# One core, S4D convolution beside a gated linear unit: the sums of two chunks of the convolution's kernels in one block of matmuls, the Fourier stage behind it, and a second Ft buffer in place of the negated sines

## The chip, the core and the metric

The kernel runs on one core of a Trainium2 chip. A core has TensorE (PE, with a separate row PEld for its weight loads), VectorE (DVE), ScalarE (ACT), GpSimd (POOL) and the queue engine SyncE (SP); each takes its instructions in a fixed order, and they wait for each other through semaphores. The metric is the device time of one execution in microseconds; three executions before the change gave a median of 730.58 us.

## The reference

With x = A_u (2048 tokens, 448 channels) and xn = layernorm(x), the result is x + A(xn) + B(xn):

```python
# A: S4D, N = 256 complex modes per channel
dt = exp(log_dt); A = -exp(log_A_real) + 1j * A_imag
C = (C_real + 1j * C_imag) * dt[:, None]
P = exp((A * dt[:, None])[:, :, None] * arange(L))
K = 2 * einsum("dn,dnl->dl", C, P).real          # a kernel of 2048 taps per channel
y = irfft(rfft(K, 2L) * rfft(u, 2L))[:L] + u * D_skip
# B: GLU
h = sigmoid(xn @ w_gate) * (xn @ w_up)           # 448 -> 1792
out_B = h @ w_down                               # 1792 -> 448
```

## The kernel before

Two streams of work share the engines. One, `glu`, is part B: 14 tiles of 128 hidden columns for two halves of the tokens, each tile a `gate` step (two groups of 11 matmuls into `gu`, then tanh `th` on ACT, `hf` on DVE, its rounded copy `hh` on ACT and the rest `hl` on DVE), and after each two or three tiles the down projection (matmuls into `po`, added into `acc` by DVE). The other, `conv`, is part A: preparation, then `kgen`, which makes the convolution kernels, then `spectra`, the Fourier products. The two are written out in turn by a table of weights (a generator yields its weight, and the one that is behind goes on); a scheduler then lays down a fixed order for each engine, in which `issue_after` puts kgen's matmuls behind the gate or down matmul written last.

The change lies in `kgen`. It works on 56 chunks of 8 channels. For a chunk, a kernel is the product of a coarse factor F (32 steps) and a fine factor E (64 steps), summed over the 256 modes (two halves of 128 partitions) and over the real and imaginary parts. For each chunk, in turn:

- `ahead`: two matmuls with `sel` make the phases in a PSUM tile `tr` (one buffer). ACT turns them into the tile S: an absolute value (L541), the sines of E and F (L542), the negated sine of E (L543, half as wide), and the cosines (L544). S has two buffers, by the chunk's parity. `ahead` of chunk c+1 is written ahead of the products of chunk c.
- `magnitudes`: POOL makes the decays `me` and `mf` for a pair of chunks in 11 products (L499, L511) out of the powers `pm` (DVE, L447); ACT squares a part (L524).
- DVE multiplies: L598 the upper 32 steps of Et, L599 the lower 32 steps, for which S is read backwards (cosine and negated sine), L600 the tile Ft. Et has two buffers by parity, Ft has one.
- 32 matmuls with Ft as weights and Et as the moving operand (L614) sum a chunk into the PSUM bank `ko`. A bank takes four chunks. The profile records each of these matmuls twice, so a chunk shows as x64.
- Once a bank is full, a matmul with `dm` adds the skip term (L624), ACT copies the bank to `ks` (L627), and `first_stage` (32 matmuls into `kp` and `kq`, L559, recorded twice as well) makes its first Fourier stage, which goes to memory as `sk_d`. With chunks counted from 0, banks fill at chunks 3, 7, 11 and so on, and their first stages are written behind chunks 6, 10, 14 and so on; the last bank's behind the last chunk.

Of the kernel before, what the change touches and what calls it, by code (L numbers as in the profile page):

```python
# [11 lines left out]
F32 = mybir.dt.float32  # L12
F32R = mybir.dt.float32r
I32 = mybir.dt.int32
AF = mybir.ActivationFunctionType
ALU = mybir.AluOpType
# [10 lines left out]
TWO_PI = 2.0 * math.pi  # L27
# [9 lines left out]
HP = 300  # L37
# [10 lines left out]
DC = 8  # L48
# [81 lines left out]
def s4d_glu_kernel(ctx, tc, io):  # L130
# [322 lines left out]
    def kgen(pk):  # L453
# [5 lines left out]
            ("S1", [128, 5, 2 * DC, 32], F32), ("Et1", [128, 2, 2 * DC, 64], F32),  # L459
            ("Et0", [128, 2, 2 * DC, 64], F32), ("Ft", [128, 2, 2 * DC, 32], F32),  # L460
            ("S0", [128, 5, 2 * DC, 32], F32), ("mf0", [128, 4 * DC, 32], F32),
# [64 lines left out]
        def ahead(cn):  # L526
# [13 lines left out]
            cs = S[:, 1:4:2]  # L540
            nc.scalar.activation(rows(cs), pv, AF.Abs)  # L541
            nc.scalar.activation(rows(S[:, 0:5:4]), pv, AF.Sin, scale=TWO_PI)  # L542
            nc.scalar.activation(rows(S[:, 2:3]), pv[:, :, 0:1], AF.Sin, scale=-TWO_PI)  # L543
# [34 lines left out]
        for g in range(NCK // NCH):  # L578
            for c in range(NCH):
# [16 lines left out]
                Ft = tl["Ft"]  # L596
                two = lambda ap: ap.unsqueeze(1).to_broadcast([128, 2, 2 * DC, 32])
                v.tensor_tensor(Et[:, :, :, 32:64], two(me[:, :, 32:64]), S[:, 1::-1], ALU.mult)  # L598
                v.tensor_tensor(Et[:, :, :, 0:32], two(me[:, :, 0:32]), S[:, 1:3, :, ::-1], ALU.mult)  # L599
                fts[:] = [v.tensor_tensor(Ft, two(mf), S[:, 3:5], ALU.mult)]  # L600
# [7 lines left out]
                with tc.issue_after(glu_mm[0].ins):  # L608
                    for q in range(2):
                        sl = 2 * (cn % 4) + q  # L610
                        for k in range(4):
                            h, cc = k // 2, k % 2
                            for j in range(4):
                                nc.tensor.matmul(  # L614
                                    ko[32 * j : 32 * j + 32, sl],
                                    Ft[:, cc, DC * h + 4 * q + j],
                                    Et[:, cc, DC * h + 4 * q + j],
                                    start=(k == 0),
                                    stop=(k == 3),
                                    skip_group_check=True,  # L620
                                )
                if cn % 4 == 3:
# [4 lines left out]
                    nc.scalar.copy(ks, ko)  # L627
                yield WK / 3
                if cn % 4 == 2 and cn > 3 or cn + 1 == NCK:

                    with hp(HP) if cn + 1 == NCK else tc.issue_after(glu_mm[0].ins):
                        first_stage((cn - 3) // 4 if cn + 1 < NCK else cn // 4)
# [527 lines left out]
```

## Time and profile before

| what | value |
|---|---|
| median of three runs | 730.58 us (728.54 to 733.38) |
| the profiled execution, own time | 727.83 us |
| its span, first to last instruction | 726.1 us |
| mean granted TensorE clock | 0.980 |
| busy: PE, PEld, DVE | 677.6, 533.8, 565.7 us |
| busy: ACT, POOL | 420.6, 384.2 us |
| matmuls of kgen's sums (L614) | from 148.1 to 536.7 us |

Busy shares are of the engine's own records. A matmul's record overlaps the next one's, so what a matmul costs is read from the distance between starts, not from its duration. What lies before 140 us is preparation and gate work, what lies behind 540 us is `spectra` with the rest of the GLU.

### The profile page before, as it was taken

The page shows a single profiled execution, that of the slowest core. Times are in us where ns is not written, and L with a number is a line of the kernel's source. Part 1 is how long each engine was busy: PE and PEld are TensorE (multiplying, and loading weights), DVE is VectorE, ACT ScalarE, POOL GpSimd, SP SyncE. Part 2 cuts the span into 40 slices and gives each one's busy share as a digit, 9 for nine tenths or more (in the row PEclk, how much of TensorE's full clock was granted, in tenths as well). Part 3 has the DMA queues.
Part 4 walks back from the last instruction along what each step waited for, and adds up shares of the span by engine and source line. Part 5 has one row for each costly group of instructions (what it writes and reads, how often), then busy time and mean ns, then how long its engine had stood idle before and what let it go on. Part 6 is the DMA issues. An engine that isn't in the chain of part 4 may idle for free.

```text
span 726.1 us, 19068 instructions
## 1 busy us (share of the span) xinstructions
PE 677.6 (93%) x7780; PEld 533.8 (74%) x7780; DVE 565.7 (78%) x776; ACT 420.6 (58%) x650; POOL 384.2 (53%) x423
## 2 busy tenths in 40 slices
PE   2898799899998999998999999999999999999994
PEld 1674688787886888655778887888877787767783
DVE  5699997699999999999499988986956555664553
ACT  3645455578787788898388678767643312323310
POOL 2110018698899988788557856767844002431001
PEclk9998899999999999999999999999999999999998
DMA  9946328525414554454952232232269999999646
GB/s 203 229 108 183 104 80 248 164 93 177 167 51 135 185 158 147 135 162 130 270 183 102 83 108 97 71 108 94 58 172 271 273 235 234 233 244 221 166 131 162
DMA packets 92710, 115.71 MB, mean 159 GB/s; under 512 B 12112, under 2 KB 81104, under 8 KB 92368
## 3 DMA queue, kind: packets, MB, share of 16 engines
q1 hardware_dynamic: 83312, 94.03, 47.2%
q10 hardware_dynamic: 6736, 14.57, 6.4%
q0 software_dynamic: 2576, 5.90, 3.3%
q8 instruction: 61, 1.00, 0.6%
q14 instruction: 25, 0.20, 0.1%
HBM read 69.70 MB, written 44.76 MB: 158 GB/s over the span
## 4 chain that ended last, share of the span: by engine, by line
PE 58%; DVE 17%; POOL 8%; DMA 7%; issue 3%; ACT 3%; SPq 2%; ACTq 0%; POOLq 0%; DVEq 0%
PE gu L706 23%; PE po L818 12%; PE sp L902 7%; PE ko L614 5%; PE pv L929 4%; POOL me L511 4%; PE tr L533 3%; DVE Et L599 2%; DVE Et L598 2%; DVE Ft L600 2%; DVE hl L724 2%; POOL mf L511 2%; DMA acc_d<-acc 1%; DVE wl L761 1%; DVE pm L447 1%
## 5 line engine op out<-in xcount | busy, mean ns | idle before, releaser
L511 POOL TENSOR_TENSOR me<-me,pm 128x32 f32<-128x32 f32 (+1 forms) x168 | 155.9, 928 | 78.1 <-DVE Et L599 65.5
L511 POOL TENSOR_TENSOR mf<-mf,pm 128x64 f32<-128x64 f32 (+1 forms) x112 | 116.5, 1040 | 4.9
L706 PE MATMUL gu<-xh,wh 128*128 128x512 f32 x336 | 101.1, 407 | 2.5 <-ACT xh L219 2.5
L706 PE MATMUL gu<-xh,wl 128*128 128x512 f32 x336 | 95.4, 392 | 0.0
L706 PE MATMUL gu<-xl,wh 128*128 128x512 f32 x336 | 95.1, 390 | 0.0
L818 PE MATMUL po<-dh,hh 128*128 128x448 f32 x224 | 86.8, 387 | 6.0 <-DVE acc L823 2.5
L598 DVE TENSOR_TENSOR Et<-me,S 128x1024 f32<-128x1024 f32 x56 | 81.8, 1460 | 7.2 <-ACT S L544 5.5
L599 DVE TENSOR_TENSOR Et<-me,S 128x1024 f32<-128x1024 f32 x56 | 79.3, 1415 | 7.8 <-ACT me L524 7.7
L818 PE MATMUL po<-dl,hh 128*128 128x448 f32 x224 | 84.5, 377 | 0.0
L541 ACT ACTIVATE S<-tr 128x1024 f32<-128x1024 f32 x56 | 57.8, 1032 | 45.3 <-PE tr L533 40.3
L600 DVE TENSOR_TENSOR Ft<-mf,S 128x1024 f32<-128x1024 f32 x56 | 78.7, 1405 | 6.8 <-ACT S L544 5.0
L818 PE MATMUL po<-dh,hl 128*128 128x448 f32 x224 | 83.7, 375 | 0.0
L706 PEld LDWEIGHTS gu<-xh,wh 128*128 128x128 f32 x336 | 62.3, 193 | 21.3 <-ACT xh L219 4.0
L722 ACT CAST hh<-hf 128x512 fp32r<-128x512 f32 x56 | 35.0, 625 | 70.0 <-DVE hf L717 57.6
L706 PEld LDWEIGHTS gu<-xh,wl 128*128 128x128 f32 x336 | 62.9, 188 | 14.9 <-DVE pl L307 0.7
L706 PEld LDWEIGHTS gu<-xl,wh 128*128 128x128 f32 x336 | 63.0, 188 | 13.9 <-issue 0.7
L614 PEld LDWEIGHTS ko<-Et,Ft 128*32 128x32 f32 x3584 | 53.8, 110 | 25.7 <-issue 14.7
L614 PE MATMUL ko<-Et,Ft 128*32 128x64 f32 x3584 | 63.9, 222 | 7.6 <-DVE Ft L600 4.2
L717 DVE SCALAR_TENSOR_TENSOR hf<-th,gu 128x512 f32<-128x512 f32 x56 | 38.2, 682 | 38.4 <-PE gu L706 28.0
L544 ACT ACTIVATE S<-S,hpi 128x1024 f32<-128x1024 f32 x56 | 65.7, 1173 | 0.0
L823 DVE SCALAR_TENSOR_TENSOR acc<-po,acc 128x448 f32<-128x448 f32 x80 | 48.5, 616 | 21.7 <-PE po L818 21.7
L724 DVE TENSOR_TENSOR hl<-hf,hh 128x512 fp32r<-128x512 f32 x56 | 51.2, 915 | 13.2 <-ACT hh L722 13.2
(196 smaller groups left out, 1286.5 us busy)
## 6 DMA issues: line engine op xcount, KB each, us to landing
sk_d<-sk ACTq DMA_DIRECT2D x14, 512.0 KB
sx<-x_d SPq DMA_DIRECT2D x32, 224.0 KB
skl<-sk_d SPq DMA_DIRECT2D x16, 448.0 KB
vp<-v_d SPq DMA_DIRECT2D x16, 448.0 KB
v_d<-vt SPq DMA_DIRECT2D x62, 112.0 KB
wt_d<-wh SPq DMA_DIRECT2D x9, 512.0 KB
wt_d<-wl SPq DMA_DIRECT2D x9, 512.0 KB
wl<-wt_d SPq DMA_DIRECT2D x9, 512.0 KB
```

The lines of the kernel that those rows point to most:

```text
L511: ins = nc.gpsimd.tensor_tensor(m[:, :, w + a : 2 * w : n], m[:, :, a:w:n], par(base + i).unsqueeze(2).to_broadcast([128, 4 * DC, w // n]) ...
L541: nc.scalar.activation(rows(cs), pv, AF.Abs)
L544: sins[:] = [nc.scalar.activation(cs, cs, AF.Sin, scale=-TWO_PI, bias=hpi)]
L598: v.tensor_tensor(Et[:, :, :, 32:64], two(me[:, :, 32:64]), S[:, 1::-1], ALU.mult)
L599: v.tensor_tensor(Et[:, :, :, 0:32], two(me[:, :, 0:32]), S[:, 1:3, :, ::-1], ALU.mult)
L600: fts[:] = [v.tensor_tensor(Ft, two(mf), S[:, 3:5], ALU.mult)]
L614: nc.tensor.matmul(ko[32 * j : 32 * j + 32, sl], Ft[:, cc, DC * h + 4 * q + j], Et[:, cc, DC * h + 4 * q + j], start=(k == 0), stop=(k == ...
L706: glu_mm[:] = [nc.tensor.matmul(ps, a_, b_, start=(n == 0), stop=(n == len(mm) - 1))]
L724: v.tensor_tensor(hl, hf, hh, ALU.subtract)
L818: glu_mm[:] = [nc.tensor.matmul(po, a_[:, bs], w_, start=(n == 0), stop=(n == 3 * fc - 1))]
L823: v.scalar_tensor_tensor(acc[:, b], po, 0.5, acc[:, b], ALU.mult, ALU.add)
L902: mm = nc.tensor.matmul(to, tb[:kk, t, 64 * c : 64 * c + 64], rhs, start=True, stop=True, skip_group_check=True,)
```

## The change

Four edits, all in kgen. The sines: S has four slots instead of five, and the negated sine is gone from ACT; the lower half of Et is made in two instructions, one product with the cosine and one `scalar_tensor_tensor` with the sine and a factor -1. Ft gets two buffers by parity, like Et. The matmuls of the sums are written only behind an odd chunk, for the even chunk before it and for itself. The first Fourier stage of a bank is written right behind the block that sums the first two chunks of the next bank, under the same anchor; the last bank's stays where it was.

```diff
-            ("S1", [128, 5, 2 * DC, 32], F32), ("Et1", [128, 2, 2 * DC, 64], F32),
-            ("Et0", [128, 2, 2 * DC, 64], F32), ("Ft", [128, 2, 2 * DC, 32], F32),
-            ("S0", [128, 5, 2 * DC, 32], F32), ("mf0", [128, 4 * DC, 32], F32),
+            ("S1", [128, 4, 2 * DC, 32], F32), ("Et1", [128, 2, 2 * DC, 64], F32),
+            ("Et0", [128, 2, 2 * DC, 64], F32), ("Ft0", [128, 2, 2 * DC, 32], F32), ("Ft1", [128, 2, 2 * DC, 32], F32),
+            ("S0", [128, 4, 2 * DC, 32], F32), ("mf0", [128, 4 * DC, 32], F32),
...
-            cs = S[:, 1:4:2]
+            cs = S[:, 1:3]
             nc.scalar.activation(rows(cs), pv, AF.Abs)
-            nc.scalar.activation(rows(S[:, 0:5:4]), pv, AF.Sin, scale=TWO_PI)
-            nc.scalar.activation(rows(S[:, 2:3]), pv[:, :, 0:1], AF.Sin, scale=-TWO_PI)
+            nc.scalar.activation(rows(S[:, 0:4:3]), pv, AF.Sin, scale=TWO_PI)
...
-                Ft = tl["Ft"]
+                Ft = tl[f"Ft{cn % 2}"]
                 two = lambda ap: ap.unsqueeze(1).to_broadcast([128, 2, 2 * DC, 32])
                 v.tensor_tensor(Et[:, :, :, 32:64], two(me[:, :, 32:64]), S[:, 1::-1], ALU.mult)
-                v.tensor_tensor(Et[:, :, :, 0:32], two(me[:, :, 0:32]), S[:, 1:3, :, ::-1], ALU.mult)
-                fts[:] = [v.tensor_tensor(Ft, two(mf), S[:, 3:5], ALU.mult)]
+                v.tensor_tensor(Et[:, 0, :, 0:32], me[:, :, 0:32], S[:, 1, :, ::-1], ALU.mult)
+                v.scalar_tensor_tensor(Et[:, 1, :, 0:32], me[:, :, 0:32], -1.0, S[:, 0, :, ::-1], ALU.mult, ALU.mult)
+                fts[:] = [v.tensor_tensor(Ft, two(mf), S[:, 2:4], ALU.mult)]
...
                 with tc.issue_after(glu_mm[0].ins):
-                    for q in range(2):
-                        sl = 2 * (cn % 4) + q
...
+                    for c_ in (cn - 1, cn) if cn % 2 else ():
+                        Et, Ft = tl[f"Et{c_ % 2}"], tl[f"Ft{c_ % 2}"]
+                        for q in range(2):
+                            sl = 2 * (c_ % 4) + q
...
+                if cn % 4 == 1 and cn > 3:
+                    with tc.issue_after(glu_mm[0].ins):
+                        first_stage((cn - 2) // 4)
                 yield WK / 3
-                if cn % 4 == 2 and cn > 3 or cn + 1 == NCK:
-
-                    with hp(HP) if cn + 1 == NCK else tc.issue_after(glu_mm[0].ins):
-                        first_stage((cn - 3) // 4 if cn + 1 < NCK else cn // 4)
+                if cn + 1 == NCK:
+                    with hp(HP):
+                        first_stage(cn // 4)
```

The order in which the instructions stand, at three places. In the rows, `ko` are the sums of a bank, `Et0` and `Et1` are the even and the odd chunk's tile, `tr` are the two phase matmuls of a later chunk, `gu` are gate matmuls; line numbers are those of each kernel's own text, so L614 before is L616 after, L706 is L710, and L598 to L600 before are L597 to L600 after, with L597 the upper half of Et, L598 and L599 the two lower parts and L600 Ft.

First place, TensorE in the second half of kgen, the odd chunk 49. Before, its sums stand alone between gate matmuls:

```order
L706 MATMUL gu_5392<-xl_3862,wh_5306 128x512 x3
L706 MATMUL gu_5436<-xh_3861,wh_5306 128x512 x3
L706 MATMUL gu_5436<-xr_3863,wh_5306 128x512
L706 MATMUL gu_5436<-xh_3861,wl_5307 128x512 x3
L706 MATMUL gu_5436<-xr_3863,wl_5307 128x512
L706 MATMUL gu_5436<-xl_3862,wh_5306 128x512 x3
L706 MATMUL gu_5488<-xh_3545,wh_5484 128x512
L614 MATMUL ko_5322<-Et1_1125,Ft_1127 32x64 x32
L533 MATMUL tr_5459<-sel_76,ph1_1133 128x512 x2
```

After, the same sums follow those of chunk 48, and the phases of chunk 50 stand five gate matmuls ahead of them:

```order
L710 MATMUL gu_5360<-xh_3897,wh_5306 128x512 x3
L710 MATMUL gu_5360<-xr_3899,wh_5306 128x512
L710 MATMUL gu_5360<-xh_3897,wl_5307 128x512 x2
L533 MATMUL tr_5348<-sel_76,ph1_1134 128x512 x2
L710 MATMUL gu_5360<-xh_3897,wl_5307 128x512
L710 MATMUL gu_5360<-xr_3899,wl_5307 128x512
L710 MATMUL gu_5360<-xl_3898,wh_5306 128x512 x3
L616 MATMUL ko_5322<-Et0_1126,Ft0_1127 32x64 x32
L616 MATMUL ko_5322<-Et1_1125,Ft1_1128 32x64 x32
```

What moved: the even chunk's sums went down by some 23 gate matmuls, to stand directly ahead of the odd chunk's.

Second place, TensorE after the change, one pair earlier (chunks 46 and 47 close a bank; `tr_5281` are the phases of the odd chunk 49):

```order
L616 MATMUL ko_4941<-Et0_1126,Ft0_1127 32x64 x32
L616 MATMUL ko_4941<-Et1_1125,Ft1_1128 32x64 x32
L626 MATMUL ko_4941<-dm_79,ident_69 128x8
L710 MATMUL gu_5260<-xh_3897,wh_5112 128x512 x3
L710 MATMUL gu_5260<-xr_3899,wh_5112 128x512
L710 MATMUL gu_5260<-xh_3897,wl_5113 128x512 x3
L710 MATMUL gu_5260<-xr_3899,wl_5113 128x512
L710 MATMUL gu_5260<-xl_3898,wh_5112 128x512 x3
L533 MATMUL tr_5281<-sel_76,ph0_1133 128x512 x2
```

What moved: before, the phases of a chunk stood a whole chunk ahead of its sums; now those of an odd chunk stand behind the previous pair's block and 11 gate matmuls, with 33 gate matmuls and one more pair of phases between them and the block that needs them.

Third place, VectorE in the first half of kgen, a pair of chunks whose decays are `me1` and `mf1` (`wl`, `hf`, `hl` belong to the GLU, `pm` are powers). Before:

```order
L599 TENSOR_TENSOR Et0_1126<-me1_1122,S0_1128 128x32x32
L761 TENSOR_TENSOR wl_3294<-wraw_2743,wh_3293 128x1024
L724 TENSOR_TENSOR hl_2733<-hf_2730,hh_2732 128x512
L598 TENSOR_TENSOR Et0_1126<-me1_1122,S0_1128 128x32x32
L600 TENSOR_TENSOR Ft_1127<-mf1_1123,S0_1128 128x1024
L447 SCALAR_TENSOR_TENSOR pm1_1180<-W1_110 128x128
L717 SCALAR_TENSOR_TENSOR hf_2822<-th_2820,gu_2808 128x512
L447 SCALAR_TENSOR_TENSOR pm1_1180<-pm1_1180 128x128
L598 TENSOR_TENSOR Et1_1125<-me1_1122,S1_1124 128x32x32
L599 TENSOR_TENSOR Et1_1125<-me1_1122,S1_1124 128x32x32
L724 TENSOR_TENSOR hl_2825<-hf_2822,hh_2824 128x512
L600 TENSOR_TENSOR Ft_1127<-mf1_1123,S1_1124 128x1024
```

After, from the GLU work behind the previous pair's last product on:

```order
L721 SCALAR_TENSOR_TENSOR hf_2460<-th_2458,gu_2446 128x512
L765 TENSOR_TENSOR wl_2708<-wraw_2485,wh_2707 128x1024
L728 TENSOR_TENSOR hl_2463<-hf_2460,hh_2462 128x512
L600 TENSOR_TENSOR Ft0_1127<-mf1_1123,S0_1129 128x1024
L447 SCALAR_TENSOR_TENSOR pm1_1180<-W1_110 128x128
L598 TENSOR_TENSOR Et0_1126<-me1_1122,S0_1129 128x16x32
L599 SCALAR_TENSOR_TENSOR Et0_1126<-me1_1122,S0_1129 128x16x32
L597 TENSOR_TENSOR Et0_1126<-me1_1122,S0_1129 128x32x32
L447 SCALAR_TENSOR_TENSOR pm1_1180<-pm1_1180 128x128
L721 SCALAR_TENSOR_TENSOR hf_2619<-th_2617,gu_2605 128x512
L599 SCALAR_TENSOR_TENSOR Et1_1125<-me1_1122,S1_1124 128x16x32
L728 TENSOR_TENSOR hl_2622<-hf_2619,hh_2621 128x512
```

What moved: Ft of the even chunk now opens the pair, behind GLU work (`hf`, `wl`, `hl`) that follows the last product of the pair before; it is the instruction that waits for TensorE to have read the even half of the previous block. A chunk takes four instructions instead of three.

22 lines of the change are left out of this document (11 added, 11 removed).

## The prediction

> **What bounds the kernel now.** I read the page first: which engine is full, and which work the chain that ended last passes through.
>
> ```profile
> span 726.1 us, 19068 instructions
> ...
> PE 677.6 (93%) x7780; PEld 533.8 (74%) x7780; DVE 565.7 (78%) x776; ACT 420.6 (58%) x650; POOL 384.2 (53%) x423
> ...
> PE 58%; DVE 17%; POOL 8%; DMA 7%; issue 3%; ACT 3%; SPq 2%; ACTq 0%; POOLq 0%; DVEq 0%
> ```
>
> TensorE is the bound of the whole, but a quarter of the chain is on DVE and POOL, so I ask where. The chain restricted to four stretches of kgen (140 to 232, 232 to 290, 290 to 372, 372 to 537 us) gives these shares by line:
>
> ```profile
> by line: POOL me L511 26.1%; POOL mf L511 12.9%; DVE Et L599 8.4%; issue 8.2%; DVE hl L724 8.1%; DVE Et L598 7.7%; DVE Ft L600 5.7%; POOL dl L788 4.6%; DVE pm L447 4.4%; DVE wl L761 4.1%; DVE hf L717 3.4%; DMA rd<-in_B_w_down_dram 3.0%; POO
> by line: PE gu L706 39.9%; PE po L818 19.9%; PE ko L614 14.9%; PE tr L533 8.4%; DVE Ft L600 4.4%; PE kp L559 3.6%; DVE hl L724 2.7%; DVE Et L598 2.2%; issue 1.8%; DVE hf L717 1.2%; DVE xt L268 1.1%; PE gu L210 1.0%; PE ko L624 0.6%; PE kq L
> by line: DMA acc_d<-acc 12.0%; DVE Et L599 10.5%; PE gu L706 8.9%; DVE Ft L600 8.8%; DVE Et L598 8.2%; PE ko L614 6.7%; issue 5.3%; PE po L818 5.2%; DVE pm L447 4.4%; PE gu L279 4.1%; DMA wl<-wt_d 4.0%; PE tr L533 3.0%; PE gu L210 2.3%; DVE
> by line: PE gu L706 41.4%; PE po L818 23.9%; PE ko L614 13.9%; PE tr L533 8.1%; PE kq L559 2.2%; PE kp L559 2.0%; DVE Et L598 1.2%; PE ko L624 1.2%; DVE Ft L600 1.1%; DVE Et L599 1.1%; ACT S L544 0.6%; ACT S L541 0.6%; ACT S L542 0.6%; issu
> ```
>
> The first and third stretch run over DVE and POOL, the second and fourth over TensorE. The busy times of the same stretches say how near the others are:
>
> ```profile
> core 0: us, PE busy (x) PEld busy (x) DVE busy (x) ACT busy (x) POOL busy (x), PEclk, DMA share, GB/s
> 140.00:232.00 92.00, 88.17 (x1239) 71.91 (x1237) 88.24 (x88) 71.25 (x104) 84.58 (x79) 1.00 0.36 122
> 232.00:290.00 58.00, 57.35 (x884) 47.20 (x887) 55.79 (x58) 47.05 (x68) 50.37 (x51) 0.97 0.50 157
> 290.00:372.00 82.00, 75.85 (x1180) 53.19 (x1168) 67.78 (x79) 64.78 (x106) 57.72 (x67) 0.98 0.60 181
> 372.00:537.00 165.00, 163.93 (x2504) 135.97 (x2502) 141.37 (x143) 119.32 (x171) 117.08 (x131) 1.00 0.32 100
> ```
>
> In the first stretch DVE is busy 88.24 of 92 us and POOL 84.58: nothing can be added there unpaid. In the last, TensorE is busy 163.93 of 165 us and DVE has 23.6 us to spare. The stretches hold 12, 9, 11 and 24 of the 56 chunks (the first sums start at 148.1 us, the last end at 536.7; I counted the blocks between).
>
> **The change, part by part.** *Fewer entries into the small matmuls.* One block of sums costs TensorE more than its matmuls. Its group, its surroundings at one place, and for comparison a pair of phase matmuls (`tr`) among gate matmuls:
>
> ```profile
> L614 PE MATMUL ko<-Et,Ft 128*32 128x64 f32 x3584 | 63.9, 222 | 7.6 <-DVE Ft L600 4.2
> ...
> 192.80 0.36 PE L818 MATMUL po<-dh,hl 128*128 128x448 f32 x1
> 193.01 0.37 PE L818 MATMUL po<-dh,hh 128*128 128x448 f32 x1
> 193.30 1.10 PE L614 MATMUL ko<-Et,Ft 128*32 128x64 f32 x64
> 194.34 0.73 PE L533 MATMUL tr<-sel,ph 128*128 128x512 f32 x2
> 194.91 0.36 PE L818 MATMUL po<-dl,hh 128*128 128x448 f32 x1
> ...
> 359.42 0.63 PE L533 MATMUL tr<-sel,ph 128*128 128x512 f32 x2
> 359.88 0.85 PE L706 MATMUL gu<-xh,wh 128*128 128x512 f32 x3
> ```
>
> Down matmuls start 0.20 us apart, so the block was due at 193.21 and starts at 193.30: 0.09 to enter. From its start to the next start are 1.04 us; its 64 records begin within 1.10 minus the last one's 0.22, so 0.88, with one step 0.90: 0.14 to leave. The phases behind it take 0.57 us, against 0.46 among gate matmuls: 0.11 more. Together 0.34 us for an entry and an exit. Two chunks in one block pay it once. Where TensorE is the chain, that is (9 + 24) / 2 = 16.5 blocks fewer, **minus 5.6 us**; in the other two stretches TensorE gets to wait earlier, and I count nothing. Moving the first Fourier stage behind a block I take as nothing: it is the same 32 matmuls, and before, each stage of the fourth stretch already stands against a block of sums; in the second, two pieces stand alone, 2 x 0.34 = 0.7 us at most.
>
> *One more instruction on DVE per chunk.* The lower half of Et becomes two instructions of 512 columns. The groups of the page and two from the view that keeps shapes apart, then least, median and longest of the instructions of S and Et (ns):
>
> ```profile
> L598 DVE TENSOR_TENSOR Et<-me,S 128x1024 f32<-128x1024 f32 x56 | 81.8, 1460 | 7.2 <-ACT S L544 5.5
> L599 DVE TENSOR_TENSOR Et<-me,S 128x1024 f32<-128x1024 f32 x56 | 79.3, 1415 | 7.8 <-ACT me L524 7.7
> L600 DVE TENSOR_TENSOR Ft<-mf,S 128x1024 f32<-128x1024 f32 x56 | 78.7, 1405 | 6.8 <-ACT S L544 5.0
> L724 DVE TENSOR_TENSOR hl<-hf,hh 128x512 fp32r<-128x512 f32 x56 | 51.2, 915 | 13.2 <-ACT hh L722 13.2
> ...
> L351 DVE TENSOR_TENSOR w<-a,b 112x512 f32<-112x512 f32 x2 | 1.4, 692 | 0.0
> L349 DVE SCALAR_TENSOR_TENSOR m<-a,b 112x512 f32<-112x512 f32 x2 | 1.4, 691 | 0.0
> ```
>
> ```profile
> L541 ACT ACTIVATE S<-tr x56: 996/1028/1084, 136.0 to 525.9; 128x1024 f32<-128x1024 f32 x56
> L542 ACT ACTIVATE S<-tr x56: 1014/1022/1082, 136.9 to 526.8; 128x1024 f32<-128x1024 f32 x56
> L543 ACT ACTIVATE S<-tr x56: 596/606/669, 137.8 to 527.7; 128x512 f32<-128x512 f32 x56
> L544 ACT ACTIVATE S<-S,hpi x56: 1136/1166/1230, 138.9 to 528.2; 128x1024 f32<-128x1024 f32 x56
> L598 DVE TENSOR_TENSOR Et<-me,S x56: 1209/1328/2099, 140.1 to 529.4; 128x1024 f32<-128x1024 f32 x56
> L599 DVE TENSOR_TENSOR Et<-me,S x56: 1207/1224/2172, 141.4 to 530.5; 128x1024 f32<-128x1024 f32 x56
> ```
>
> Undisturbed, 1024 columns take 1.21 us (the minima), 512 take 0.69 us for either operation: 2 x 0.69 - 1.21 = 0.17 us more. That is on the chain in the first and third stretch, 12 + 11 = 23 chunks: **plus 3.9 us**. In the fourth, 24 x 0.17 = 4.1 us lie in DVE's 23.6 idle us.
>
> The means lie above the minima because DVE and POOL hold each other up:
>
> ```profile
> 189.70 1.33 DVE L600 TENSOR_TENSOR Ft<-mf,S 128x1024 f32<-128x1024 f32 x1
> ...
> 189.91 2.04 POOL L511 TENSOR_TENSOR me<-me,pm 128x512 f32<-128x512 f32 x1
> ...
> 190.96 1.15 DVE L447 SCALAR_TENSOR_TENSOR pm<-W 128x128 f32<-128x128 f32 x1
> ```
>
> POOL's product starts under Ft and ends late; then a DVE product of 128 columns, which shares no data with it, takes 1.15 us. The excess per instruction is about the same for 1024 columns (1415 - 1207 = 208 ns) as for 512 (915 - 691 = 224 ns). So a fourth instruction might cost another 0.2 us: 23 x 0.2 = 4.6 us. Or nothing, since POOL's work doesn't grow and it may only slip in at another place. I take the middle, **plus 2.3 us**.
>
> *ACT sheds the negated sine.* 56 x 0.61 = 34 us less work, and each S is there 0.61 us earlier. What DVE waits for from 140 to 372 us bounds its worth (total, times, longest, in us):
>
> ```profile
> DVE Et L598 <- ACT S L544: 3.2, 5, 1.3
> ...
> DVE Et L599 <- ACT me L524: 2.5, 4, 0.8
> ...
> DVE Ft L600 <- PE ko L614: 0.4, 1, 0.4
> ```
>
> Of the 3.2 us I take half, **minus 1.5 us**. The last row prices the second Ft on its own: DVE waited 0.4 us for the single one in this part, so it brings nothing by itself; what it does is allow the pair.
>
> *The pair as a barrier.* New waits come in two places. The even Ft of the next pair waits for TensorE to have read the even half of this block; queued behind it on DVE are the rest of the pair and the GLU's `hf` and `hl`. Between the last product of a pair and that Ft, the order has two or more instructions of the GLU and of `pm`, `hl` with its 0.92 us mostly among them, which cover the 0.9 us of the even half. I price it at nothing while they last, and at up to 0.9 us a pair without them; in the last stretch that would lie in DVE's idle time, in the first its 6 pairs would pay 5.4 us, which I put beside the collisions' 4.6 us for the high end, not on top: where DVE stands, POOL has its turn.
>
> The other is on TensorE, behind which the gate matmuls queue: the odd chunk's phases now stand 33 gate matmuls and a pair of phases ahead of the block, 33 x 0.23 + 2 x 0.46 = 8.5 us (a gate matmul is as wide as a phase matmul: 0.46 / 2), and the odd sums start 0.9 us later, 9.4 us. In that time fit: phases 0.46, ACT 1.03 + 1.02 + 1.17 = 3.2, DVE's odd Et and Ft at their minima 0.69 + 1.21 + 0.69 + 1.21 = 3.8; 7.5 us; the first part of Et can overlap the cosine, but an instruction of the GLU stands between on ACT and one or two on DVE. One collision with POOL of 0.87 us (2.08 against 1.21) is covered, two or three aren't. In the fourth stretch, 12 pairs: between nothing and one whole uncovered collision each, 10.4 us. I take 0.2 us a pair, nearer to nothing, since TensorE seldom waited for the sums' tiles before (8 times in all of kgen):
>
> ```profile
> PE ko L614 <- DVE Ft L600: 4.2, 6, 2.2
> PE ko L614 <- DVE Et L598: 3.4, 2, 1.8
> ```
>
> **Plus 2.4 us.** The sum is -5.6 + 3.9 + 2.3 - 1.5 + 2.4 = **+1.5 us** on the span of 726.1 us, whose execution took 727.83 us by itself; the median of the runs lies 2.75 us above that, and I put the same difference on it: 730.6 + 1.5 = **732.1 us**.
>
> The place to weigh a rule is the collision. The Trainium skill, page "SBUF — State Buffer", section "Who interferes with whom", says that a DVE instruction with two SBUF inputs and a GpSimd instruction that reads SBUF exclude each other, whichever starts second being blocked for the whole of the other. The 1.15 us of the 128-column product agree. By that rule every added start on DVE is a new chance to be blocked; the rival below works that out from rows.
>
> **The rivals.** *TensorE's gain whole* (0.25): the fourth instruction hides in POOL's own pauses and S comes early enough. For it: POOL's products keep their number, and POOL's lines are 39% of the first stretch's chain, DVE's Et and Ft 22%. Then -5.6 - 1.5 leaves 723.5 us, and -5.6 - 3.2 = -8.8, 722 us, if all of the waits for S go too.
>
> *The barrier decides, slower* (0.20): in the fourth stretch each pair's odd products end after the 9.4 us, and TensorE stands with the gate matmuls behind it. It decides once two of a pair's collisions fall behind the odd phases. For it: DVE's maxima of 2.1 us, and TensorE's own fullness, which leaves a stall no place to hide; against it: DVE's 14% of idle time there. Price: -5.6 + 3.9 + 4.6 + 10.4 = +13.3, 744 us.
>
> *Every added start is blocked* (0.10): 0.22 us (the 224 ns above) at each of the 23 chunks on the chain, with the 0.17 there 9.0 us; -5.6 + 9.0 + 2.4 - 1.5 = +4.3, 735 us. This is what the rule just named would make of the split.
>
> *The block is not made whole*, other work standing between its halves, would undo the 5.6 us and leave 737.7 us; the order after speaks against it except in the third stretch, where I count none, so I give it no chance of its own.
>
> **How the numbers follow.** The forecast has 0.45, its own range is 727 to 738. The range for 8 in 10 reaches from the rival below, 722, to the barrier's full price, 744. A measurement of this kernel tells about 1% from no change, which is 723.3 to 737.9 us. Faster by more: 0.15 of the whole-gain rival and 0.01 of the forecast, 0.16. Slower by more: 0.18 of the barrier, 0.05 of the blocked starts, 0.04 of the forecast, 0.27. The rest, 0.57, lies within.
>
> **What would show it.** In the profile after: blocks of sums as x128 with about 1.9 us to the next start; ACT's busy time some 34 us lower; DVE's split products near 0.69 us at the least, 0.8 to 0.9 in the mean; the chain from 372 us on still on TensorE. I am wrong if TensorE's idle time before the sums from 372 to 530 us is above 5 us (then the barrier holds), or if the first stretch gets shorter than its 92 us although DVE has more to do there (then POOL, not DVE, held it).

## The result and the profile after

The change made the kernel slower: 761.5 us (median of 6 runs, 757.2 to 768.9) against 731.3 us (6 runs) on the same chip, a ratio of 1.040 with a 95% interval of 1.036 to 1.044. Forecast were 732.1 us and a range of 722 to 744. Executions over 1.5% above the fastest of the same kernel are left out of the ratios here and below, among them the profiled one of the change (768.9 us at a mean granted clock of 0.945, against 0.954 to 0.963 in the other five) and one of the kernel before that took 2127 us. The profiled execution of the change lies 7.4 us above the median, so some 7 of the 41.0 us that follow belong to that execution and not to the change.

From the page of the changed kernel: span, busy times, granted clock in 40 slices, the chain by engine, and the groups of the sums and of the new product on DVE (busy time, mean ns of one, then the idle time ahead of the group and what ended it).

```profile
span 767.1 us, 19043 instructions
...
PE 689.5 (90%) x7780; PEld 549.3 (72%) x7780; DVE 581.3 (76%) x832; ACT 397.7 (52%) x594; POOL 363.8 (47%) x423
...
PEclk9898899989999999896899999999899999989998
...
PE 56%; DVE 19%; ACT 7%; DMA 6%; issue 5%; POOL 3%; SPq 2%; ACTq 1%; DVEq 0%; POOLq 0%
...
L616 PE MATMUL ko<-Et,Ft 128*32 128x64 f32 x3584 | 62.9, 227 | 19.8 <-DVE Ft L600 19.8
...
L599 DVE SCALAR_TENSOR_TENSOR Et<-me,S 128x512 f32<-128x512 f32 x56 | 57.7, 1030 | 21.2 <-ACT S L542 21.1
```

The span grew by 41.0 us. TensorE is idle for 767.1 - 689.5 = 77.6 us of it, before for 48.5: 29.1 us more. The other 11.9 us are busy time, although TensorE has the same matmuls to do: the granted clock is lower in many slices. It now stands 19.8 us before the sums, waiting for Ft, where it stood 7.6 us before, 4.2 of them for Ft. DVE in turn stands 21.1 us before its new product, waiting for ACT's S.

Where this happens is read from the start of the sums of chunks 0, 12, 21, 32 and 55, the bounds of the four stretches. Before they start at 148.1, 232.3, 296.1, 381.1 and 535.8 us, after at 151.0, 240.4, 304.5, 413.7 and 573.2. So the start is 2.9 us later, the first stretch 5.2 longer, the second 0.3, the third 24.2, the fourth 4.8, and what lies behind 3.6; together 41.0. These are not yet the losses of the stretches, because the new order has also laid other gate work between the same chunks: 161, 99, 176 and 286 gate matmuls (L710) in the four stretches, where L706 had 180, 110, 135 and 294. At the 0.23 us that the prediction takes for one, 41 more are 9.4 of the third stretch's 24.2 us, and the 30 that the first two no longer hold hide 6.9 us of loss there. Nearer to the loss is the time that TensorE stands. The busy times of the changed kernel in its own four stretches, with bounds set against these starts as in the view of before (columns as there):

```profile
core 0: us, PE busy (x) PEld busy (x) DVE busy (x) ACT busy (x) POOL busy (x), PEclk, DMA share, GB/s
...
140.00:240.00 100.00, 90.12 (x1210) 74.89 (x1210) 96.20 (x104) 68.99 (x93) 86.17 (x88) 0.95 0.31 107
240.00:298.00 58.00, 53.02 (x821) 45.22 (x820) 53.69 (x61) 37.44 (x53) 43.00 (x46) 0.94 0.46 151
298.00:404.00 106.00, 91.99 (x1283) 67.60 (x1282) 72.94 (x95) 69.43 (x108) 51.51 (x68) 0.89 0.53 159
404.00:574.00 170.00, 160.44 (x2485) 136.04 (x2487) 148.84 (x167) 107.79 (x144) 111.96 (x130) 0.98 0.30 97
```

TensorE stands 9.9, 5.0, 14.0 and 9.6 us, before 3.8, 0.7, 6.2 and 1.1, and the clock fell from 1.00, 0.97, 0.98 and 1.00 to 0.95, 0.94, 0.89 and 0.98. This is not the mark of one long execution alone: in the run `cross_single` of the next part, whose profiled execution took 755.8 us, TensorE stands 11.3, 4.2, 8.5 and 9.3 us between the starts of the same sums (9.9, 6.9, 12.1 and 9.6 in the change), and the third stretch takes 108.7 us. A pause of TensorE costs twice, as the timeline of one pair's block and the windows around it show:

```profile
164.28 1.10 PE L616 MATMUL ko<-Et,Ft 128*32 128x64 f32 x64
169.05 1.94 PE L616 MATMUL ko<-Et,Ft 128*32 128x64 f32 x64 [3.67 <-DVE Ft L600]
```

```profile
168.00:170.00 2.00, 0.95 (x36) 0.95 (x40) 2.00 (x3) 1.34 (x2) 1.92 (x2) 0.50 0.00 0
170.00:172.00 2.00, 2.00 (x44) 1.73 (x33) 2.00 (x3) 0.45 (x1) 2.00 (x2) 0.50 0.04 12
172.00:174.00 2.00, 2.00 (x6) 1.59 (x5) 2.00 (x3) 2.00 (x4) 2.00 (x4) 0.50 0.48 159
174.00:176.00 2.00, 2.00 (x9) 1.62 (x8) 2.00 (x3) 1.58 (x2) 2.00 (x3) 0.91 0.66 204
```

The odd half of the block waits 3.67 us for its Ft, while DVE is busy throughout (2.00 of 2.00 us); the clock falls to 0.50 during the wait and stays there until about 174.4, and the 64 records of the odd half take 1.94 us where those of the even half took 1.10. Some 5.4 us at half the clock behind 3.67 us of standing are up to 2.7 us more, an estimate.

### The profile page after: what moved, and what is told of

Read it like the earlier page. It is cut to its first block, busy times and chain, and to the rows that moved or that the text cites. A ratio compares the mean times of both kernels' runs of the same rounds, so it can differ in the third digit from the quotient of the medians.

```text
span 767.1 us, 19043 instructions
## 1 busy us (share of the span) xinstructions
PE 689.5 (90%) x7780; PEld 549.3 (72%) x7780; DVE 581.3 (76%) x832; ACT 397.7 (52%) x594; POOL 363.8 (47%) x423
## 4 chain that ended last, share of the span: by engine, by line
PE 56%; DVE 19%; ACT 7%; DMA 6%; issue 5%; POOL 3%; SPq 2%; ACTq 1%; DVEq 0%; POOLq 0%
PE gu L710 25%; PE po L822 10%; PE sp L906 7%; PE ko L616 4%; PE pv L933 4%; DVE Ft L600 4%; DVE Et L598 2%; DVE Et L597 2%; DVE Et L599 2%; PE tr L533 2%; ACT S L543 2%; PE kp L558 1%; DVE pm L447 1%; DVE hf L721 1%; DVE wl L765 1%
## 5 line engine op out<-in xcount | busy, mean ns | idle before, releaser
L511 POOL TENSOR_TENSOR me<-me,pm 128x32 f32<-128x32 f32 (+1 forms) x168 | 149.4, 889 | 121.4 <-DVE Et L598 95.8
L710 PE MATMUL gu<-xh,wh 128*128 128x512 f32 x336 | 104.3, 421 | 5.0 <-ACT xh L219 3.5
L511 POOL TENSOR_TENSOR mf<-mf,pm 128x64 f32<-128x64 f32 (+1 forms) x112 | 107.0, 956 | 2.1
L710 PE MATMUL gu<-xh,wl 128*128 128x512 f32 x336 | 99.3, 402 | 0.0
L822 PE MATMUL po<-dh,hh 128*128 128x448 f32 x224 | 89.0, 397 | 9.2 <-DVE acc L827 6.0
L710 PE MATMUL gu<-xl,wh 128*128 128x512 f32 x336 | 96.8, 396 | 0.0
L600 DVE TENSOR_TENSOR Ft<-mf,S 128x1024 f32<-128x1024 f32 x56 | 76.5, 1367 | 11.0 <-ACT S L543 5.4
L597 DVE TENSOR_TENSOR Et<-me,S 128x1024 f32<-128x1024 f32 x56 | 79.4, 1418 | 3.5 <-ACT S L543 3.5
L710 PEld LDWEIGHTS gu<-xh,wh 128*128 128x128 f32 x336 | 64.3, 200 | 23.9 <-ACT xh L219 5.1
L616 PE MATMUL ko<-Et,Ft 128*32 128x64 f32 x3584 | 62.9, 227 | 19.8 <-DVE Ft L600 19.8
L616 PEld LDWEIGHTS ko<-Et,Ft 128*32 128x32 f32 x3584 | 55.5, 114 | 32.7 <-DVE Ft L600 22.0
L710 PEld LDWEIGHTS gu<-xh,wl 128*128 128x128 f32 x336 | 65.3, 195 | 16.0 <-DVE pl L307 0.7
L710 PEld LDWEIGHTS gu<-xl,wh 128*128 128x128 f32 x336 | 64.3, 192 | 14.7 <-issue 0.7
L599 DVE SCALAR_TENSOR_TENSOR Et<-me,S 128x512 f32<-128x512 f32 x56 | 57.7, 1030 | 21.2 <-ACT S L542 21.1
L822 PEld LDWEIGHTS po<-dh,hh 128*128 128x128 f32 x224 | 45.3, 202 | 22.0 <-DVE acc L827 7.2
```

Of the source, the lines that this page charges most:

```text
L511: ins = nc.gpsimd.tensor_tensor(m[:, :, w + a : 2 * w : n], m[:, :, a:w:n], par(base + i).unsqueeze(2).to_broadcast([128, 4 * DC, w // n]) ...
L599: v.scalar_tensor_tensor(Et[:, 1, :, 0:32], me[:, :, 0:32], -1.0, S[:, 0, :, ::-1], ALU.mult, ALU.mult)
L600: fts[:] = [v.tensor_tensor(Ft, two(mf), S[:, 2:4], ALU.mult)]
L616: nc.tensor.matmul(ko[32 * j : 32 * j + 32, sl], Ft[:, cc, DC * h + 4 * q + j], Et[:, cc, DC * h + 4 * q + j], start=(k == 0), stop=(k == ...
L710: glu_mm[:] = [nc.tensor.matmul(ps, a_, b_, start=(n == 0), stop=(n == len(mm) - 1))]
L822: glu_mm[:] = [nc.tensor.matmul(po, a_[:, bs], w_, start=(n == 0), stop=(n == 3 * fc - 1))]
```

## The experiments

All times are medians beside runs of the kernel before on the same chip (730.6 to 732.3 us). Idle is the span less TensorE's busy time in the profiled execution, clock its mean granted clock.

| run | pair | split | Ft | us | ratio to before (95%) | idle | clock |
|---|---|---|---|---|---|---|---|
| before | no | no | 1 | 731 | | 48.5 | 0.980 |
| the change | yes | yes | 2 | 761.5 | 1.040 (1.036 to 1.044) | 77.6 | 0.945 |
| split_only | no | yes | 2 | 757.5 | 1.036 (1.031 to 1.041) | 66.1 | 0.954 |
| pair_unsplit | yes | no | 2 | 750.7 | 1.025 (1.020 to 1.030) | 70.3 | 0.962 |
| cross_single | part | yes | 2 | 758.1 | 1.037 (1.032 to 1.042) | 68.9 | 0.958 |
| single_unsplit | no | no | 2 | 753.5 | 1.029 (1.023 to 1.034) | 63.4 | 0.960 |
| one_ft_unsplit | no | no | 1 | 734.7 | 1.006 (1.003 to 1.010) | 54.9 | 0.981 |
| one_ft_split | no | yes | 1 | 746.7 | 1.022 (1.015 to 1.028) | 62.8 | 0.968 |
| stage_new | no | no | 1 | 742.7 | 1.016 (1.011 to 1.021) | 58.0 | 0.966 |
| pair_from_32 | part | yes | 1, 2 | 744.6 | 1.018 (1.010 to 1.026) | 65.0 | 0.971 |
| even_single_unsplit | no | no | 2 | 760.1 | 1.037 (1.034 to 1.041) | 69.9 | 0.966 |
| even_split_only | no | yes | 2 | 764.1 | 1.041 (1.036 to 1.046) | 69.8 | 0.956 |
| even_before | no | no | 1 | 753.4 | 1.030 (1.025 to 1.034) | 66.8 | 0.961 |
| even_one_ft_split | no | yes | 1 | 757.7 | 1.034 (1.030 to 1.037) | 71.1 | 0.961 |
| late3_split | no | yes | 2 | 748.8 | 1.024 (1.020 to 1.028) | 65.3 | 0.970 |
| late2_split | no | yes | 2 | 762.6 | 1.044 (1.038 to 1.049) | 70.3 | 0.968 |
| late3_single | no | no | 2 | 743.6 | 1.017 (1.013 to 1.021) | 57.9 | 0.969 |
| late1_before | no | no | 1 | 743.4 | 1.018 (1.013 to 1.022) | 57.6 | 0.970 |
| rows_single | no | no | 2 | 727.0 | 0.993 (0.990 to 0.996) | 46.1 | 0.978 |
| rows_split | no | yes | 2 | 729.8 | 0.998 (0.995 to 1.001) | 50.3 | 0.979 |

**First: the parts of the change.** The pairing taken out of the change (the first stage goes back to its old place):

```diff
-                    for c_ in (cn - 1, cn) if cn % 2 else ():
+                    for c_ in (cn,):
```

> The changed kernel without the pairing: sums per chunk and the first Fourier stage at its old place, with the split of Et's lower half, the sine no longer negated on ACT, and two Ft. If the pair is a barrier and holds the loss (theory 1), this stays near the kernel before: +3.9 for the split, up to +4.6 for collisions, -1.5 for S, so 727 to 738 us. If the fourth instruction on DVE and its collisions with POOL hold it (theory 2), 750 us or more.

757.5 us: without any pair 26 of the 30 us remain. Theory 1, that the pair holds the loss, falls. TensorE waits for the sums' tiles all the same; its rows between 140 and 410 us, and below them those of the kernel before:

```profile
PE ko L616 <- DVE Ft L600: 11.7, 5, 4.0
PE ko L616 <- DVE Et L597: 3.8, 3, 2.1
```

```profile
PE ko L614 <- DVE Ft L600: 3.4, 5, 2.2
PE ko L614 <- DVE Et L598: 3.4, 2, 1.8
```

The pair kept, the split undone:

```diff
-                v.tensor_tensor(Et[:, 0, :, 0:32], me[:, :, 0:32], S[:, 1, :, ::-1], ALU.mult)
-                v.scalar_tensor_tensor(Et[:, 1, :, 0:32], me[:, :, 0:32], -1.0, S[:, 0, :, ::-1], ALU.mult, ALU.mult)
+                v.tensor_tensor(Et[:, :, :, 0:32], two(me[:, :, 0:32]), S[:, 1::-1, :, ::-1], ALU.mult)
```

> The changed kernel with the pairs and the moved stage, but Et's lower half in one DVE instruction of 1024 columns. The sign of the sine is left out of the computation there, so that three instructions a chunk do, as before; ACT sheds the negated sine as in the change. Theory 1 (pair as a barrier): most of the 30 us stay, 750 to 762 us. Theory 2 (split and collisions): 725 to 735 us.

750.7 us: most of the loss stays without the split as well. Pairs everywhere but at the switch of the GLU's halves:

```diff
-                    for c_ in (cn - 1, cn) if cn % 2 else ():
+                    for c_ in (cn,) if 20 <= cn < 32 else (cn - 1, cn) if cn % 2 else ():
```

> The changed kernel, but with sums per chunk for chunks 20 to 31, those of the switch between the GLU's halves; pairs elsewhere. The start of the sums of chunk 31 fell back 30 us in the change, 21 of them between chunks 22 and 31. If those 21 us come from the pair meeting the work of the switch, this gives 738 to 746 us. If the pair costs the same everywhere and the switch only shows it, 12 of 56 chunks give back some 6 us: 752 to 758 us.

758.1 us, which neither time nor interval tells from the change or from the run without pairs. The sums of chunk 32 start at 403.9 us in it, at 413.7 in the change, but those of chunk 0 start 7.8 us earlier already, and the third stretch, now without pairs, takes 108.7 us against 109.2: its growth isn't the pairs' meeting with the switch. Last, no pairs and no split, both edits above at once:

> As the run with the split alone, but Et's lower half in one DVE instruction, the sign of the sine left out of the computation: no pairs, no split, the stage at its old place; what is left is ACT without the negated sine, and two Ft. By the prediction's terms -1.5 to -3.2 us and no more: 727 to 731 us. If ACT's 34 us were worth more on the chain, below 724 us. Its difference to the run with the split alone is the price of the split, which I put at 3.9 to 8.5 us.

753.5 us, a miss of 22 us, for a kernel that does *less* than the one before: the same products, the same sums, no negated sine. Neither theory was left. What distinguishes it from the kernel before is ACT's missing instruction and the second Ft.

**Second: the second Ft, and edits one at a time.** One Ft in place of two:

```diff
-                Ft = tl[f"Ft{cn % 2}"]
+                Ft = tl["Ft"]
```

> The kernel before with nothing changed but ACT's negated sine gone (S in four slots, Et's lower half in one DVE instruction, the sign of the sine left out of the computation). It differs from the run without pairs and split in one thing: a single Ft instead of two. Theory A (new): with one Ft the sums of a chunk can't be laid down closely behind those of the chunk before, since Ft has to be made anew in between; the second Ft takes that spacing away, the scheduler sets blocks side by side, and TensorE waits for DVE. Then this run gives back the 22 us: 722 to 733 us. Theory B: the order is upset by ACT's missing sine itself: 745 us or more, like its sibling's 753.5.

> The change's sines and split products, with a single Ft, sums per chunk, the stage at its old place. Theory A: 727 to 740 us, against 757.5 with two Ft; its difference to the run with one Ft and the unsplit product is the price of the split, 3.9 to 8.5 us by the prediction. Theory B: 748 us or more.

734.7 and 746.7 us. So a second buffer alone, by which no instruction becomes faster or slower, costs 18.8 us without the split and 10.8 with it, and the split 12.0 with one Ft and 4.0 with two. Costs that change so much with what else is there are hardly the edits' own. What an edit changes beside its instructions is the order that the scheduler lays down: with two Ft TensorE's order has the sums of chunks 2 to 9 as 39, 0, 27, 0, 31, 0, 34 and 0 gate or down matmuls behind the sums ahead of them, before as 30, 23, 3, 29, 31, 23, 9 and 22. The moved stage by itself is the clearest case, since not one instruction is added or removed:

```diff
                 if cn % 4 == 3:
...
+                if cn % 4 == 1 and cn > 3:
+                    with tc.issue_after(glu_mm[0].ins):
+                        first_stage((cn - 2) // 4)
                 yield WK / 3
-                if cn % 4 == 2 and cn > 3 or cn + 1 == NCK:
...
```

> The kernel before with nothing changed but the place of the first Fourier stage: right behind the sums of the first chunk pair of the next bank, as in the change. The prediction priced this move at nothing (at most -0.7 us): 728 to 734 us. If the order laid down is what decides, it may come out otherwise, since 735 rows of TensorE's order stand elsewhere: above 740 us would show that.

742.7 us, 12 us for nothing but other places. Its page (span, busy times) and its longest wait of TensorE for kgen between 140 and 410 us (total, times, longest):

```profile
span 743.3 us, 19058 instructions
...
PE 685.3 (92%) x7780; PEld 540.1 (73%) x7780; DVE 565.8 (76%) x776; ACT 422.3 (57%) x650; POOL 380.6 (51%) x423
```

```profile
PE ko L614 <- DVE Ft L600: 9.9, 5, 3.2
```

DVE's busy time is that of before (565.7), TensorE's 7.7 us longer at a clock of 0.966. Pairs from chunk 32 on only, with one Ft and single sums ahead of that:

> The change's sines and split with one Ft and sums per chunk up to chunk 31, and pairs with two Ft from chunk 32 on, where TensorE is the bound; the stage at its old place. By the prediction's terms the pairs gain 12 x 0.34 = 4.1 us there less the barrier's 2.4 against the run with one Ft and split. If pairs make TensorE stand there as well (in the change, chunks 32 to 55 took 159.5 us against 154.7 before), it is 2 to 5 us slower than that run.

744.6 against 746.7 us without pairs, with intervals that overlap widely (1.010 to 1.026 and 1.015 to 1.028): what pairs cost or gain in the stretch where TensorE is full is too small to be told here.

**Third: even spacing.** If sums set side by side were the harm, gate and down matmuls that may not overtake the sums written ahead of them would mend it. `ko_mm` collects the last matmul of each chunk's sums; the same is done for the down matmuls:

```diff
-            with tc.issue_after(sp_mm[0].ins) if glu_on else nullcontext():
+            with tc.issue_after(sp_mm[0].ins) if glu_on else tc.issue_after(ko_mm[-1].ins) if len(ko_mm) > 0 else nullcontext():
```

> The run without pairs and split (two Ft, 753.5 us; the sign of the sine is left out of the computation as there), with one thing added: gate and down matmuls that are written behind a chunk's sums also stay behind them on TensorE, so that the sums stand in the order in which they are written, mostly 22 gate or down matmuls apart, where that run had 39, 0, 27, 0, 31, 0, 34, 0. Theory A (two Ft let the scheduler set sums side by side, and that costs): 730 to 740 us, the 19 us come back although both Ft are there. Theory C (the second Ft costs by itself, by its place in memory or by what DVE does with it): 748 us or more.

> The same on the run with split and two Ft, without pairs (757.5 us). Theory A: 735 to 748 us. The difference to the run above is the price of the split where the order of TensorE's work is the same in both: the prediction's 3.9 to 8.5 us if the split costs by its instructions, up to 12 as between the two runs with one Ft.

> The kernel before with the same spacing, nothing else. Its sums stand 20 to 30 matmuls apart already, with a few closer (3, 9, 4), so theory A expects little: 725 to 735 us. If holding the gate matmuls back behind the sums itself costs, 740 us or more, and then the two runs above carry that cost too.

> The same spacing on the run with the split and one Ft (746.7 us). Theory A: with even spacing one and two Ft are alike, so within 4 us of the run with split, two Ft and even spacing. If one Ft holds DVE up (it must wait for TensorE to read it), slower than that run.

760.1, 764.1, 753.4 and 757.7 us: theory A falls. The kernel before itself, with its own instructions and evenly spaced sums, is 21 us slower (1.030, 1.025 to 1.034). Its waits of TensorE between 140 and 410 us:

```profile
PE tr L533 <- ACT S L543: 11.9, 5, 5.3
PE ko L614 <- DVE Et L598: 5.6, 4, 2.3
PE ko L614 <- DVE Ft L600: 5.4, 4, 2.1
```

The sums wait 11.0 us here, against 6.8 in the kernel before, and the phases (`tr`) 11.9, against none. So gate work that runs ahead of the sums looks like the cover under which DVE and ACT make their tiles; that reading is argued from these waits, not tried by itself.

**Fourth: later sums.** So perhaps the sums stand too early. Two buffers of Et and Ft allow to write them up to a whole chunk later (`late3`; a third of a chunk is one yield of kgen). `sums` holds the matmuls of a chunk's block, as they were:

```diff
+                if cn:
+                    sums(cn - 1)
                 yield WK / 3
```

> The run with split and two Ft (757.5 us), with the sums of a chunk written a whole chunk later, behind the products of the next chunk, which the two buffers of Et and Ft allow; the first stages follow. Theory D (the sums stand too early among the gate work, and TensorE stands with gate matmuls queued behind them): TensorE's waits before the sums of the first 24 chunks fall from 16 us to under 6, its granted clock rises from 0.954 to above 0.97, and the time falls to 730 to 742 us. Theory E (DVE's chain is what is longer; order only shows it): DVE now waits for TensorE to read Et and Ft, and the time stays at 750 us or more.

> The same, but the sums written two thirds of a chunk later, right behind the products of the next chunk. Theory D: between the run above and 757.5, nearer to the run above: 733 to 748 us. Theory E: 750 us or more.

> The run without pairs and split, two Ft (753.5 us; the sign of the sine left out of the computation), with the sums a whole chunk later. Theory D: 725 to 737 us, below the 734.7 of the run with one Ft if the waits vanish wholly. Theory E: 748 us or more.

> The kernel before with its sums written one third of a chunk later, ahead of the products of the next chunk; one Ft, which then waits for them. Theory D: little to gain, since TensorE waits only 4.7 us before the sums of the first 24 chunks; 726 to 733 us. If one Ft makes DVE wait for the later sums, 738 us or more.

748.8, 762.6, 743.6 and 743.4 us. A whole chunk later gains 9 to 10 us over the same kernels with the sums at the end of their own chunk, less than theory D promised; two thirds gain nothing; and the kernel before loses 12 us by a third. What took the place of the waits shows in the run `late3_split` between 140 and 410 us:

```profile
PE po L834 <- DVE acc L839: 5.2, 3, 3.5
PE tr L533 <- ACT S L542: 4.8, 5, 1.4
PE ko L581 <- DVE Ft L634: 3.5, 3, 2.0
PE gu L279 <- DVE xr L223: 3.1, 1, 3.1
```

The sums' wait for Ft fell from the 11.7 us quoted above to 3.5, as D had it; other waits came instead. One rule for the place of the sums doesn't explain the order's price.

**Fifth: the order of before.** The question that was left can be put directly. The n-th instruction that the edited kernel writes for an engine is the n-th of the kernel before, if the negated sines are struck out there; so a table can give every engine of the edited kernel the very order of rows that it has in the kernel before (a second split product goes right behind the first). `_ROWS` holds that list of instruction numbers for each engine, and edges that bind only the issue order, without a wait, tie each row to the next:

```diff
         s4d_glu_kernel(tc, io)
+        _keep_rows(nc, tc)
...
+def _keep_rows(nc, tc):
+    seen = {i.name: i for i in nc.cur_bb.bb.instructions}
+    for text in _ROWS.values():
+        last = None
...
+                    tc.add_manual_dep(
+                        seen[name], last,
+                        mybir.DependencyInfo(mybir.DependencyClass.NoSync, mybir.DependencyReason.DATA),
+                        reason="issue_after",
+                    )
```

> The run without pairs and split, with two Ft (753.5 us; the sign of the sine left out of the computation), and every engine's rows tied to the order that they have in the kernel before, the negated sine simply missing. Theory F (the loss is the order): the prediction's terms for what is left, ACT's relief of -1.5 to -3.2 us and nothing for the second Ft, hold: 726 to 732 us. Theory E (the second Ft and the missing sine cost by themselves): 745 us or more.

> The run with split and two Ft, without pairs (757.5 us), with every engine's rows in the order of the kernel before, the second split product right behind the first. Theory F: the split's own price on top of the run above, 3.9 to 8.5 us by the prediction, less where it hides: 729 to 740 us. Theory E: 750 us or more.

727.0 and 729.8 us. The traces show that the order is the same: TensorE's 7780 records follow each other in both as in the kernel before, and so do DVE's and POOL's but for the second split product, and ACT's but for the negated sines. With the order held, the 26.5 and 27.7 us are gone, and two Ft, S without the negated sine and the split together are as fast as the kernel before (0.998, 0.995 to 1.001), 32 us faster than the change. The page of the run with the split:

```profile
span 728.4 us, 19042 instructions
...
PE 678.1 (93%) x7780; PEld 534.5 (73%) x7780; DVE 578.8 (79%) x832; ACT 395.8 (54%) x594; POOL 370.0 (51%) x423
...
PEclk9998999998999999998999999999999999999998
```

and of the one without:

```profile
span 723.4 us, 18986 instructions
...
PE 677.3 (94%) x7780; PEld 533.9 (74%) x7780; DVE 567.6 (78%) x776; ACT 396.0 (55%) x594; POOL 386.4 (53%) x423
...
PEclk9998899999999999998999999999999999999998
```

TensorE is busy for 678 us as before, not 689 to 693, and idle for 50 and 46 us. Theory F is shown for these edits: their loss is the order. Three things stay open. Pairs and the moved stage are changes of TensorE's order themselves, and an order of before in which only the even sums or only the stage are moved was not run; in free orders they moved the time from 757.5 to 761.5 us with the split and from 753.5 to 750.7 without, both within overlapping intervals. All engines were tied at once, SyncE with its transfers too, so which engine's order carries the loss is not separated. And which property of the order of before makes it good is not known; neither even spacing nor lateness of the sums brought the time back.

## Why the prediction was wrong

**The step that failed** is that the sum has no term for the new order of all the other rows. It shows in the part on entries, "in the other two stretches TensorE gets to wait earlier, and I count nothing", and in the same nothing for the moved stage. All terms were priced on the order of before, at three places where I had read the new one. But the edits re-laid the rows of all engines: TensorE stands 38.4 us in the four stretches where it stood 11.7, also in the fourth, which was to stay full (9.6 against 1.1), and its clock fell behind these pauses. That re-laying alone is worth 12 us (the stage moved, nothing else), 21 us (even spacing, nothing else) and 26.5 and 27.7 us (the same instructions in the scheduler's order and in that of before).

The terms one by one:

- *Entries, -5.6.* The size was right as work. The rows of a pair in the changed kernel, a block and the matmul that follows it:

```profile
467.81 1.99 PE L616 MATMUL ko<-Et,Ft 128*32 128x64 f32 x128
469.74 0.27 PE L558 MATMUL kp<-wk,ks 64*64 64x64 f32 x1
```

  From start to next start 1.93 us, forecast 1.9. And in the two runs without split, with and without pairs, at clocks of 0.962 and 0.960, TensorE is busy for 680.2 and 690.4 us: 10.2 less, where 28 blocks at 0.34 us make 9.5. As time it can't be told from nothing (750.7 against 753.5).

- *Split, +3.9 and +2.3 for collisions.* With the order held, 729.8 - 727.0 = 2.8 us, which the first term covers; the collisions didn't show. The two products (least, median, longest in ns) in the run with the order held:

```profile
L598 DVE TENSOR_TENSOR Et<-me,S x56: 673/684/1640, 139.2 to 532.2; 128x512 f32<-128x512 f32 x56
```

```profile
L599 DVE SCALAR_TENSOR_TENSOR Et<-me,S x56: 677/794/1636, 139.9 to 532.8; 128x512 f32<-128x512 f32 x56
```

  One of them is undisturbed in the median, the other 0.12 us over its least. DVE is busy for 578.8 - 567.6 = 11.2 us more, 0.20 a chunk, against 0.17 worked out without collisions. In the change the second has a mean of 1.03 us, above the 0.8 to 0.9 that I gave. The rival by which every added start is blocked for 0.22 us is not borne out where the order is the same.

- *ACT's relief, -1.5.* Right in sign and too small: the run without split and with the order held, which has the second Ft as well, is 0.7% faster (0.4 to 1.0%), 3 to 7 us; the 3.2 that I had as the bound lie at the lower end. ACT's busy time fell by 22.9 us in the change, not by the 34 of the line; ACT's records overlap (before, their durations add up to 477.6 us, its busy time to 420.6).

- *The second Ft, nothing.* Right with the order held: it is in that faster run. In a free order it cost 18.8 us.

- *The moved stage, nothing.* Wrong: 12 us in a free order, for the reason above.

- *The pair as a barrier, +2.4.* About right in its place. TensorE's waits in the changed kernel's fourth stretch (404 to 565 us), and those for the sums' tiles in the first three (140 to 404 us):

```profile
PE po L822 <- DVE acc L827: 3.5, 1, 3.5
PE ko L616 <- DVE Ft L600: 2.4, 2, 2.2
PE kp L558 <- issue: 2.3, 1, 2.3
PE kq L558 <- issue: 1.4, 1, 1.4
```

```profile
PE ko L616 <- DVE Ft L600: 17.4, 8, 3.7
```

  I had set 5 us from 372 us on as the mark of a barrier that holds; 2.4 us are below it. The other 7.2 us of the fourth stretch, before the down projection and the first Fourier stages, had no term. The 17.4 us lie where I had counted nothing, and 15.5 us of such waits (11.7 for Ft, 3.8 for Et) are there without any pair. The rival of the barrier, 744 us, had the right sign, but put its price into the fourth stretch, which grew by 4.8 us; the whole gain (722) and the block not made whole (737.7) didn't come about.

- *The first stretch* didn't get shorter than before (84.2 us to 89.4 between the sums of chunks 0 and 12, with 19 gate matmuls fewer in it), as forecast; the mark told nothing of the 30 us.

The sum for the edits that could be tried with the order held was +3.9 + 2.3 - 1.5 = +4.7 us; measured are -1.4 (-3.4 to +0.6). The local terms were off by 6 us, the prediction by 29.

## What to carry to other kernels

Where a scheduler lays down the order, an edit has two prices, its own and that of the new order, and the second can be many times the first: here -1 us and 28 for what could be tried. Read the whole order, not only the places of the edit, and try an edit with the old order tied down before judging it; an edit that costs nothing in the old order and much in the new one has lost to the order, not to its own instructions. And a stretch in which the bounding engine "only waits" was not free here: its pauses were lost, and part of the clock behind them too.

## What the runs showed of the hardware that was not expected

TensorE's granted clock halves behind short pauses. In 20 traces of these runs I took each pause of TensorE between 140 and 600 us that began at a clock of 1.00 and looked as far as 6 us behind it: the clock fell in 5 of 33 cases for pauses of 1.2 to 1.5 us, in 26 of 61 for 1.5 to 2.4, in 8 of 13 for 2.4 to 2.7, and in 49 of 51 above.

How the pause lies on a grid tells the cases apart. In each of these traces the clock changes only at moments a multiple of 3.41 us apart. Of the windows of that grid at a clock of 1.00 (same 20 traces, 140 to 600 us), all 65 in which TensorE was busy for less than 40% were followed by one at half the clock, 12 of 21 between 40 and 50%, and 20 of 2448 above. Two pairs of neighbours in the kernel before, the first window of each with a pause of 1.79 and of 2.24 us, and the four windows around the pause of 3.67 us in the change:

```profile
174.95:178.36 3.41, 1.62 (x67) 1.08 (x66) 3.41 (x6) 2.64 (x5) 3.17 (x4) 1.00 0.42 120
178.36:181.77 3.41, 3.41 (x17) 2.85 (x16) 3.41 (x3) 3.41 (x6) 3.41 (x2) 1.00 0.48 180
229.57:232.98 3.41, 1.18 (x77) 1.07 (x80) 3.31 (x4) 3.41 (x5) 3.17 (x5) 1.00 0.75 274
232.98:236.39 3.41, 3.41 (x70) 2.47 (x59) 3.12 (x2) 2.59 (x4) 3.33 (x3) 0.50 0.03 5
```

```profile
164.12:167.53 3.41, 1.26 (x65) 0.94 (x64) 3.41 (x4) 2.95 (x5) 3.33 (x3) 1.00 0.50 185
167.53:170.94 3.41, 1.89 (x65) 1.72 (x65) 3.41 (x4) 1.81 (x3) 3.33 (x4) 0.50 0.05 18
170.94:174.35 3.41, 3.41 (x13) 2.83 (x10) 3.41 (x5) 2.80 (x4) 3.41 (x4) 0.50 0.38 124
174.35:177.76 3.41, 3.41 (x16) 2.79 (x16) 3.41 (x4) 1.68 (x3) 3.41 (x5) 1.00 0.60 176
```

The first number behind the length is TensorE's busy time, the first one behind the last bracket the clock: 1.62 of 3.41 us busy left it at 1.00, 1.18 and 1.26 did not.

The Trainium skill, page "TensorE: Matmul & The Clock Gate", section "Part 1: The HAM clock gate (the "warmup" mystery)", says that TensorE falls to half its clock after an idle window of about 3.4 us, with windows that run freely, and comes back after about as long a time of work. The half clock agrees (0.50 in the windows above), and so does the length of the window (3.41 us), by which the same pause sometimes costs and sometimes doesn't. But here the window need not be idle: pauses well below 3.4 us were enough, in 34 of 74 cases between 1.5 and 2.7 us. The measurement decides, and a pause of 2 us on TensorE should be priced with the clock behind it.
